# A result buffer of its own for the out product, stored by ACT, in a chunked recurrence with a gated convolution behind it

## The chip, the core and the metric

The kernel runs on one core of a Trainium2 chip. The core has five engines, each with an instruction stream that it works through in order: TensorE (PE, with its weight loads shown apart as PEld), VectorE (DVE), ScalarE (ACT), GpSimd (POOL) and SyncE (SP). Transfers between the chip's memory and the core's, and inside the core's memory, are issued by SP, ACT or POOL and carried by 16 DMA engines. The metric is the device time of one execution in microseconds (us), lower is better.

## The reference, cut to what matters

```python
# B, H, S, D = 4, 8, 768, 40
for t in range(S):
    y[:, :, t] = einsum('bhd,bhde->bhe', r_t, state)
    Sa = einsum('bhde,bhe->bhd', state, a_t)
    state = state * w_t - outer(Sa, b_t) + outer(v_t, k_t)
x = y.transpose(0, 2, 1, 3).reshape(B, S, 320)
gate = sigmoid(causal 5-tap convolution of x along S, per channel)
out = (gate * (x @ w_val)) @ w_out          # (B, S, 320)
```

All data is fp32. A recurrence over 768 steps for 32 heads, and behind it, per time step, a convolution with a sigmoid and two 320 x 320 products.

## The kernel before

**The recurrence** is cut into 24 chunks of 32 steps. A chunk c first has work that needs only its inputs (loads `ew`, scans, the matrices `am`, a triangular solve on DVE for four chunks at a time, lines 427 to 462). Then comes the serial part, chunk after chunk: `u0` on PE (lines 512 to 520) needs the state of the chunk before; ACT copies it into `ub` (523); `ut` and `u` on PE (525 to 533); ACT evacuates them into `vu` and `w` (536, 540); `g` on PE (544); the products `ysa` and `ysb` (553); DVE takes the new state out of them (563) and the results y into the buffer `xe` (577).

**The part behind it** ("the gated part") works on groups of two chunks, 0-1, 2-3, ... to 20-21, and on the single chunks 22 and 23. For group c (named by its first chunk) the steps are: `xd`, twelve transfers inside the core that move y from `xe` into the layout of the products, `xt` (`x_moves`, lines 72 to 80, issued at 705); the convolution `cv` (ACT at 725, DVE at 727) into `ag`; the gate (737 to 742); the product `val` in three parts (PE, lines 90 and 98; DVE at 757 multiplies by the gate); the product `out`, one for each half of the group (108); `os`, ACT's copy of the result out of the accumulator (772); and `store`, the transfer to the output (776). The gated part of a group runs some chunks behind the recurrence, in between its steps.

**Buffers.** `xt` has two halves (`XTW`, lines 287 and 288), used by groups in turn, so the moves of group c write the half that group c - 4 used. The copy `os` of a group writes into that group's own half of `xt`, which its convolution and its product `val` no longer need (line 720, `xo = (XTW, ...)`), and `store` reads it there. `xe` has two halves as well (line 280): before chunk c's y can be written, DVE's copy `new_xe` (572) puts the last four columns of the group before in front, and it has to wait until the moves of group c - 4 have read that half. `td` and `DB` belong to the solve of the first four chunks alone; `DB` lies in the second half of `xt`.

**What sets the order.** Every step is an operation of a `Plan` with an engine, a planned duration, the operations it waits for and a latency. `Plan.order` (lines 166 to 262) places them on the five engines with planned times, and the instructions of each engine are written out in that order. The order is fixed when the kernel is built; on the chip each engine waits at each instruction for the semaphores of its data. So a step that comes late holds everything behind it on its engine. The moves of group c wait in the plan for `("store", pg, 0)` and `("store", pg, 1)` of group pg = c - 4 (line 708). Moves and stores of the groups up to chunk 22 stand on POOL, 560 ns planned for a move, 850 for a store, 2200 for landing; those of chunk 23 partly on SP (line 707). A semaphore that tells that a transfer has landed is one of eight that the transfers of POOL use in turn, and of eight others that those of SP and ACT share in turn; before one is used again the transfer that used it last has to have landed.

```python
xo = (XTW, gi % 2 * 680) if tail < 0 else (fk[tail], 0)
...
op(("os", c, j), "ACT", ac(DM), om, osc)
...
op(("store", c, j), mq[0], mq[2], [("os", c, j)], store, 2200)
```

Of the kernel before, what the change touches and what calls it, by code (L numbers as in the profile page):

```python
# [9 lines left out]
F32 = mybir.dt.float32  # L10
# [6 lines left out]
B, H, S, D = 4, 8, 768, 40  # L17
C = 32
P16 = 16
ER = 104  # L20
DM = 320
# [11 lines left out]
TWO = 1  # L33
# [11 lines left out]
def ac(n):  # L45
    return 154 + 0.833 * n
# [106 lines left out]
class Plan:  # L153
# [6 lines left out]
    def op(self, name, eng, dur, deps, fn, lat=None, give=None):  # L160
        assert name not in self.ops, name
        self.ops[name] = [eng, dur, list(deps), fn, LAT if lat is None else lat]
        if give:
            self.gives[name] = list(give)
# [100 lines left out]
def fast_path(ctx, tc, ins, out, nch, cst, wts, wz, wmx):  # L265


    nc = tc.nc
    V, A, G, T = nc.vector, nc.scalar, nc.gpsimd, nc.tensor
    const = ctx.enter_context(tc.tile_pool(name="const", bufs=1))  # L270
# [3 lines left out]
    ch = ctx.enter_context(tc.tile_pool(name="ch", bufs=2))  # L274
# [12 lines left out]
    XTW = const.tile([128, 2 * 680], F32, name="xt")  # L287
    XT = [XTW[:, i * 680:(i + 1) * 680].rearrange("p (b t) -> p b t", b=10) for i in range(2)]
    DB = XTW[:, 680:1192].rearrange("p (u z s) -> p u z s", z=2, s=C)
    AG = const.tile([128, 2 * 646], F32, name="ag")  # L290
    ind = const.tile([ER, P16, 33], F32, name="ind")
    ern = const.tile([ER, P16, C], F32, name="er")
# [9 lines left out]
    st_ = {}  # L302
    plan = Plan()
    op = plan.op

    sg, groups = [], []
    c = 0
    while c < nch:
        n = min(nch - c, 4)
        sg.append((c, n))  # L310
        c += n
    c = 0
    while c < nch:
        n = 2 if c + 2 < nch else 1
# [8 lines left out]
    def B2(nm, c):  # L323
        return (nm, c, 0), (nm, c, 1)
# [16 lines left out]
    op("bz", "POOL", 1100, [], lambda: G.memset(UB, 0.0))  # L341
    op("nz", "POOL", 3000, [], lambda: [G.memset(x, 0.0) for x in NB + [DB, Q1]])
    op("ez", "SP", 2400, [("load", 6)], lambda: dma(RE.rearrange("p u x -> p (u x)"), ins["re"]), 2500)
# [114 lines left out]
                        in1=maskL.unsqueeze(1).to_broadcast([128, 8, C]), op=ALU.mult)  # L458

    def end2(g):  # L460
        td = st_["td", g] = ch.tile([128, P16, 4, 8], F32, name="td", bufs=1)
        V.transpose(out=td.rearrange("p s c u -> p (s c u)"), in_=st_["x", g][:, 0:P16].rearrange("p s t -> p (s t)"))

    def nblock(c, z):
# [3 lines left out]
    def dblock(c, z):  # L468
        g, c4 = sof[c]
        A.activation(out=DB[:, :, z, 0:P16], in_=st_["td", g][:, :, c4, :].rearrange("p s u -> p u s"), func=AF.Copy, scale=own[:, z:z + 1])  # L470

# [8 lines left out]
    def stage_q2(c, s):  # L480
        for j, i in JI:
            T.matmul(out=s[hr(i), 128 + j * C:160 + j * C], lhsT=DB[hr(i), j].rearrange("p z s -> p (z s)"), rhs=Q1[hr(i), j], start=True, stop=True)

# [98 lines left out]
    for c in range(nch):  # L582
        q = c - NQ
        g, c4 = sof[c]
# [87 lines left out]
    wl = None  # L672
    for i in range(NWT // WB):
# [7 lines left out]
        wl = [("wc", i, 7)]  # L681
# [9 lines left out]
    wl = wl + ["wzc"]  # L691
    prev_gv, prev_out = list(wl), list(wl)
    wv, wo, cw = weights(wts, wz)
    for gi, (c, n) in enumerate(groups):
        L = n * C
        w = B * L
        fk = [KB[(nch + x) % NQ].rearrange("p u d -> p (u d)") for x in range(-NQ, 4 - NQ)]
        tail = gi - len(groups) + 2
        xt = XT[gi % 2] if tail < 0 else fk[tail][:, 0:360].rearrange("p (b t) -> p b t", b=10)
        pg = groups[gi - 2][0] if gi > 1 else -1  # L700
        f = n / 2.0

        def xd(hf, c=c, xt=xt, L=L, last=tail > 0):
            for o, i in x_moves(xt, st_["xe", c], L, hf):
                (nc.sync if last and hf else G).dma_start(out=o, in_=i)  # L705
        last = tail > 0
        mq = ("SP", 860, 650) if last else ("POOL", 560, 850)
        xw = [x for j in range(n) for x in B2("evac_y", c + j)] + wl + [("cv", pg, 4, 0), ("cv", pg, 4, 1), ("cv", pg, 4, 2), ("val", pg, 2), ("store", pg, 0), ("store", pg, 1)]
        if tail >= 0:
            xw = B2("evac_y", c)  # L710
        for hf in range(2):
            op(("xd", c, hf), mq[0] if hf else "POOL", (7 * 560, 4 * mq[1])[hf], xw, lambda hf=hf, xd=xd: xd(hf), 2200)
        xds = [("xd", c, 0), ("xd", c, 1)]
        op(("xd", c), "SP", 1, xds, lambda: None, 2200)
        ag, go = (AG, 640) if tail < 0 else (fk[2 if tail else 3], 320)
        acc, gv = [ag[:, i * go:i * go + 10 * L].rearrange("p (b t) -> p b t", t=L) for i in range(2)]
        gf = ag[:, go:go + 10 * L]
        if tail >= 0:
            prev_gv, prev_out = [], []
        xo = (XTW, gi % 2 * 680) if tail < 0 else (fk[tail], 0)  # L720

        def cv(i, k, xt=xt, L=L, acc=acc):
            q = slice(4 * k, min(4 * k + 4, 10))
            if i == 0:
                A.mul(out=acc[:, q], in_=xt[:, q, 0:L], mul=cw[:, k, 0:1])  # L725
            else:
                V.scalar_tensor_tensor(out=acc[:, q], in0=xt[:, q, i:i + L], scalar=cw[:, k, i:i + 1], in1=acc[:, q],  # L727
                                       op0=ALU.mult, op1=ALU.add)
        for k in range(3):
            for i in range(5):  # L730
                op(("cv", c, i, k), "DVE" if i else "ACT", 70 + (270 if k < 2 else 135) * f + 45, ([("cv", c, i - 1, k)] if i else xds + wl + prev_gv), lambda i=i, k=k, cv=cv: cv(i, k))

        parts = [(0, 4, (0,)), (4, 8, (1,)), (8, 10, (2,))] if c + n == nch else [(0, 10, (0, 1, 2))]
        for i, (q0, q1, ks) in enumerate(parts):
            f_ = f * (q1 - q0) / 10
            a_, g_ = acc[:, q0:q1], gv[:, q0:q1]
            op(("abs", c, i), "ACT", 90 + 535 * f_, [("cv", c, 4, k) for k in ks] + prev_out, lambda a_=a_, g_=g_: A.activation(out=g_, in_=a_, func=AF.Abs))
            op(("gexp", c, i), "ACT", 90 + 535 * f_, [("abs", c, i)], lambda g_=g_: A.activation(out=g_, in_=g_, func=AF.Exp, scale=-1.0))
            op(("gln", c, i), "ACT", 90 + 535 * f_, [("gexp", c, i)], lambda g_=g_: A.activation(out=g_, in_=g_, func=AF.Ln, bias=1.0))
            op(("max", c, i), "DVE", 70 + 670 * f_, [("gln", c, i)],  # L740
               lambda a_=a_, g_=g_: V.scalar_tensor_tensor(out=a_, in0=a_, scalar=0.0, in1=g_, op0=ALU.min, op1=ALU.subtract))
            op(("gate", c, i), "ACT", 90 + 535 * f_, [("max", c, i)], lambda a_=a_: A.activation(out=a_, in_=a_, func=AF.Exp))
        gates = [("gate", c, i) for i in range(len(parts))]
        prev_gv, vm = [], []
        vx = [w, w, w // 2]
        late = c + n == nch

        when = [("u0", c + 3), ("u", c + 3), ("ysb", c + 3, 1), ("u0", c + 4), ("ysb", c + 4, 1)]
        for m in range(3):
            def val(m=m, c=c, xt=xt, L=L, vx=vx):  # L750
                val_mms(nc, slot(("val", c, m))[:, 0:vx[m]], wv, xt, m, L)
            op(("val", c, m), "PE", (1450 if m < 2 else 820) * f, xds + wl + vm + ([] if late else gates + [when[m]]), val, give=[("gv", c, m)])
            vm = [("val", c, m)]
        for m in range(3):
            def gvm(m=m, c=c, L=L, acc=acc, gv=gv, vx=vx):
                q = slice(4 * m, min(4 * m + 4, 10))
                V.tensor_tensor(out=gv[:, q], in0=slot(("val", c, m))[:, 0:vx[m]].rearrange("p (b t) -> p b t", t=L),  # L757
                                in1=acc[:, q], op=ALU.mult)
            op(("gv", c, m), "DVE", dv(256 * f if m < 2 else 128 * f, 1), [("val", c, m)] + gates, gvm)
            prev_gv.append(("gv", c, m))  # L760
        om = []
        prev_out = []
        for j in range(n):
            def outm(j=j, c=c, n=n, gf=gf):
                out_mms(nc, slot(("out", c, j))[:, 0:DM], gf, wo, j, n)
            nm = ("out", c, j)
            op(nm, "PE", 1980, prev_gv + om + ([] if late else [when[3 + j]]), outm, give=[("os", c, j)])
            om = [nm]
            prev_out.append(nm)

            def osc(j=j, c=c, xo=xo):
                A.copy(out=xo[0][:, xo[1] + j * DM:xo[1] + (j + 1) * DM], in_=slot(("out", c, j))[:, 0:DM])  # L772
            op(("os", c, j), "ACT", ac(DM), om, osc)

            def store(j=j, c=c, n=n, L=L, xo=xo, last=last):
                (nc.sync if last else G).dma_start(out=out[j * B // n:(j + 1) * B // n, c * C:c * C + L], in_=xo[0][:, xo[1] + j * DM:xo[1] + (j + 1) * DM])  # L776
            op(("store", c, j), mq[0], mq[2], [("os", c, j)], store, 2200)

    A.preload_act_table_set("natural_log_exp_and_others")
    E_ = mybir.EngineType  # L780
# [168 lines left out]
```

## Time and profile before

| | us |
|---|---|
| time, median of 3 runs (lowest to highest) | 543.69 (542.23 to 549.13) |
| the profiled execution's own time | 543.18 |
| its span in the trace | 541.3 |
| PE busy | 423.7 |
| DVE busy | 378.6 |
| ACT busy | 316.1 |
| POOL busy | 103.4 |

The span is the time from the first instruction of the trace to the last; the rest of the execution's own time lies around it. Busy time counts no waiting and no issuing of loads by SP. The rows below are whole lines of the profile's page and of answers from the trace. In a timeline a row gives the start, the length, the engine, the line, what was done and how often; in brackets stands the idle time of that engine just before, and what ended it. In the chain of work that ended last, read backwards from the end, each piece is what the next one waited for.

### The profile page before, as it was taken

Reading aid. Unit: us, or ns where it says so; the run is one execution under the profiler, and the core shown is the slowest. Engines: PE = TensorE matmul, PEld = TensorE weight load, DVE = VectorE, ACT = ScalarE, POOL = GpSimd, SP = SyncE. Lnnn points to the kernel's source line nnn. Section 1 sums busy time; section 2 is a strip of 40 time slices with the busy share of each in tenths; the row PEclk is TensorE's granted clock in tenths of the full one; section 3 lists DMA queues with packets and bytes.
Section 4 is the critical chain, followed back from the end, with each engine's and each line's share of the span. In section 5 each row is a group of like instructions: output and inputs, shape, how many; then the busy total and the mean of one; then the engine's idle time right before and its main releaser. Section 6 shows DMA issues by size and latency. Waiting matters only on the chain.

```text
span 541.3 us, 22177 instructions
## 1 busy us (share of the span) xinstructions
PE 423.7 (78%) x9769; PEld 364.2 (67%) x9769; DVE 378.6 (70%) x935; ACT 316.1 (58%) x644; POOL 103.4 (19%) x187
## 2 busy tenths in 40 slices
PE   4707669879769979897983996985987988998790
PEld 3707669778759768777872876774876766776660
DVE  4548946887999988796994695994795746443430
ACT  3636455657867769685684485676464527562530
POOL 3000000040310140032031023013014051338410
PEclk8766756888869999897996898997999697999696
DMA  8855733474664646647355526441252352341101
GB/s 179 199 134 135 188 85 90 100 172 111 152 152 99 146 118 136 154 112 164 86 130 133 145 49 154 87 113 29 78 105 60 66 124 59 96 90 35 37 17 38
DMA packets 24262, 58.96 MB, mean 109 GB/s; under 512 B 10953, under 2 KB 15215, under 8 KB 21665
## 3 DMA queue, kind: packets, MB, share of 16 engines
q1 hardware_dynamic: 13169, 49.52, 39.1%
q0 software_dynamic: 10992, 7.97, 6.3%
q8 instruction: 78, 1.28, 1.1%
q14 instruction: 23, 0.19, 0.1%
HBM read 49.25 MB, written 3.93 MB: 98 GB/s over the span
## 4 chain that ended last, share of the span: by engine, by line
PE 42%; DMA 18%; issue 17%; DVE 11%; ACT 6%; POOL 5%; POOLq 0%; ACTq 0%; DVEq 0%
DMA out<-xt 6%; PE pf L90 5%; PE pc L553 4%; PE pf L389 4%; DMA xt<-xe 4%; PE pf L108 4%; DMA ew<-in_ew 4%; PE pf L419 4%; PE pc L532 4%; PE pf L544 4%; POOL xt L705 4%; PE pc L515 3%; PE pc L519 3%; PE pc L528 3%; DMA ag<-in_wts 1%
## 5 line engine op out<-in xcount | busy, mean ns | idle before, releaser
L705 POOL DMA_DIRECT2D xt<-xe x132 | 68.0, 521 | 199.9 <-DVE tm L443 113.7
L727 DVE SCALAR_TENSOR_TENSOR ag<-xt,wts,ag 128x256 f32<-128x256 f32 (+1 forms) x132 | 53.6, 431 | 10.7 <-ACT ag L725 10.6
L776 POOL DMA_DIRECT2D out<-xt x22 | 18.2, 827 | 218.7 <-ACT xt L772 211.6
L389 PE MATMUL pf<-kb,qb 104*64 104x64 f32 x768 | 34.8, 260 | 30.7 <-DVE kb L384 22.8
L389 PEld LDWEIGHTS pf<-kb,qb 104*64 104x64 f32 x768 | 31.9, 172 | 33.0 <-ACT er L356 16.0
L445 DVE TENSOR_TENSOR x<-x,tm 128x58 f32<-128x58 f32 (+9 forms) x164 | 51.4, 314 | 0.6
L443 DVE TENSOR_TENSOR tm<-x 128x58 f32<-128x58 f32 (+9 forms) x164 | 51.3, 313 | 0.6
L108 PE MATMUL pf<-wts,ag 128*128 128x320 f32 x132 | 47.6, 482 | 1.0 <-DVE ag L757 1.0
L544 PE MATMUL pf<-rb,vu 104*64 104x64 f32 x768 | 33.0, 248 | 17.6 <-DVE ak L408 12.3
L544 PEld LDWEIGHTS pf<-rb,vu 104*64 104x64 f32 x768 | 29.2, 159 | 22.2 <-DVE ak L408 12.7
L540 ACT COPY w<-pc 32x640 f32<-32x640 f32 x48 | 32.9, 685 | 17.4 <-PE pc L532 16.9
L351 DVE TENSOR_TENSOR_SCAN lam<-ew,ind 104x528 f32<-104x528 f32 x24 | 30.0, 1248 | 16.8 <-DMA ew<-in_ew 16.7
L532 PE MATMUL pc<-ub,T 64*32 64x80 f32 x768 | 37.4, 254 | 5.3 <-issue 5.3
L553 PE MATMUL pc<-re,s 40*40 40x72 f32 x1472 | 33.1, 231 | 8.3 <-ACT s L422 4.6
L523 ACT ACTIVATE ub<-pc,cst 128x320 f32<-128x320 f32 x48 | 22.7, 522 | 28.0 <-PE pc L519 28.0
L532 PEld LDWEIGHTS pc<-ub,T 64*32 64x32 f32 x768 | 31.9, 121 | 7.8 <-issue 6.5
L380 ACT ACTIVATE qb<-qa,cst 104x512 f32<-104x512 f32 x48 | 32.5, 714 | 7.4 <-DVE qa L377 7.3
L503 ACT ACTIVATE rb<-rv,cst 104x512 f32<-104x512 f32 x48 | 34.5, 719 | 1.9 <-DMA rv<-in_rv 1.6
L553 PEld LDWEIGHTS pc<-re,s 40*40 40x40 f32 x1472 | 27.1, 117 | 12.5 <-ACT s L422 5.0
L553 PE MATMUL pc<-w,kbt 64*40 64x72 f32 x1536 | 33.3, 232 | 1.9 <-DVE w L547 1.1
L419 PE MATMUL pf<-cst,kb 104*128 104x104 f32 x192 | 28.7, 290 | 7.2 <-DVE kb L384 4.3
L528 PE MATMUL pc<-T,ub 64*40 64x32 f32 x1536 | 23.5, 212 | 13.1 <-issue 11.9
(119 smaller groups left out, 952.3 us busy)
## 6 DMA issues: line engine op xcount, KB each, us to landing
ew<-in_ew SPq DMA_DIRECT2D x24, 838.5 KB
rv<-in_rv SPq DMA_DIRECT2D x24, 624.0 KB
w<-in_vw SPq DMA_DIRECT2D x48, 144.0 KB
va<-in_va SPq DMA_DIRECT2D x24, 160.0 KB
out<-xt POOLq DMA_DIRECT2D x22, 160.0 KB, 7.0
xt<-xe POOLq DMA_DIRECT2D x66, 42.5 KB, 5.0
ag<-in_wts SPq DMA_DIRECT2D x5, 323.0 KB
re<-in_re SPq DMA_DIRECT2D x1, 468.0 KB
```

The source lines that it names most:

```text
L108: T.matmul(out=ps, lhsT=gv[r, q * L:q * L + 128], rhs=wo[k][r], start=(k == 0), stop=(k == 2))
L389: T.matmul(out=s[hr(i), j * 64:j * 64 + 64], lhsT=QB[c % NQ][:, pj(j, i)].rearrange("p z t -> p (z t)"), rhs=st_["kb", c][:, pj(j, i)].rea ...
L419: T.transpose(out=s[:, b * 128:b * 128 + ER], in_=src[:, u:u + 2].rearrange("p i f -> p (i f)"), identity=ident[0:ER, 0:ER])
L443: V.tensor_tensor(out=tv, in0=x[:, :, j:j + 1, r].to_broadcast(sh), in1=x[:, :, 0:j, j:j + 1].to_broadcast(sh), op=ALU.mult)
L445: V.tensor_tensor(out=x[:, :, 0:j, r], in0=x[:, :, 0:j, r], in1=tv, op=ALU.subtract)
L503: A.activation(out=st_["rb", c][:, :, z], in_=st_["rv", c][:, 0], func=AF.Copy, scale=ownz[:, z:z + 1])
L528: T.matmul(out=PC[0][hr(z, 40), i, j * C:j * C + C], lhsT=UB[hr(i), j, z], rhs=st_["T", c][hr(i), j], start=True, stop=True)
L532: T.matmul(out=PC[1][i * 64 + 32:i * 64 + 64, j // 4, j % 4 * 80:j % 4 * 80 + 80], lhsT=st_["T", c][hr(i), j], rhs=UB[hr(i), j].rearrange( ...
L544: T.matmul(out=s[hr(i), j * 64:j * 64 + 64], lhsT=st_["vu", c][:, pj(j, i)].rearrange("p x t -> p (x t)"), rhs=st_["rb", c][:, pj(j, i)].r ...
L553: T.matmul(out=PC[g][hr(z, 40), i, j % 4 * 72:j % 4 * 72 + 72], lhsT=l[hr(i, k), j * 2 + z], rhs=rhs[hr(i, k), j * 2 + z], start=start and ...
L705: (nc.sync if last and hf else G).dma_start(out=o, in_=i)
L727: V.scalar_tensor_tensor(out=acc[:, q], in0=xt[:, q, i:i + L], scalar=cw[:, k, i:i + 1], in1=acc[:, q], op0=ALU.mult, op1=ALU.add)
```

## The change

`os` gets a buffer `OS` of its own, with one half for each chunk of a group, used by every group of two chunks; a group's copy waits for the store of the same half of the group before (`po`). All stores are issued by ACT, planned at 400 ns, where they were on POOL (the last one on SP). The moves no longer wait for stores. `td` moves into the first half of `xt`, and so the first group's moves wait for its last readers (`db`), the second group's for the last reader of `DB` (`q2`).

```diff
+    OS = const.tile([128, 2 * DM], F32, name="os")
...
-        td = st_["td", g] = ch.tile([128, P16, 4, 8], F32, name="td", bufs=1)
+        td = st_["td", g] = XTW[:, 0:512].rearrange("p (s c u) -> p s c u", s=P16, c=4)
...
-        xw = [... + wl + [("cv", pg, 4, 0), ("cv", pg, 4, 1), ("cv", pg, 4, 2), ("val", pg, 2), ("store", pg, 0), ("store", pg, 1)]
+        xw = [... + wl + [("cv", pg, 4, 0), ("cv", pg, 4, 1), ("cv", pg, 4, 2), ("val", pg, 2)]
+        if gi == 0:
+            xw += [("db", x, z) for x in range(sg[TWO][0]) for z in range(2)]
+        if gi == 1:
+            xw += [("q2", sg[TWO][0] - 1)]
...
-        xo = (XTW, gi % 2 * 680) if tail < 0 else (fk[tail], 0)
+        xo = (OS, 0) if tail < 0 else (fk[tail], 0)
+        po = groups[gi - 1][0] if gi and tail < 0 else -1
...
-            op(("os", c, j), "ACT", ac(DM), om, osc)
+            op(("os", c, j), "ACT", ac(DM), om + [("store", po, j)], osc)
...
-                (nc.sync if last else G).dma_start(out=out[...], in_=xo[0][...])
-            op(("store", c, j), mq[0], mq[2], [("os", c, j)], store, 2200)
+                A.dma_start(out=out[...], in_=xo[0][...])
+            op(("store", c, j), "ACT", 400, [("os", c, j)], store, 2200)
```

The order of POOL's instructions around one group, before: four moves that end a group's twelve, the two stores (`out<-xt`, line 776) of the group two back, and the first moves of the next group. DMASW0 to DMASW7 are POOL's eight landing semaphores.

```order
L705 DMA xt<-xe 40x272 [waits DMASW3_49]
L776 DMA out<-xt 2x64x320 [waits DMASW4_49,Activation_49]
L776 DMA out<-xt 2x64x320 [waits DMASW5_49,Activation_49]
L705 DMA xt<-xe 40x272 [waits DMASW4_49,DMASW6_49,DVE_49,PE_49]
L705 DMA xt<-xe 40x272 [waits DMASW7_49]
L705 DMA xt<-xe 8x272 [waits DMASW0_49]
L705 DMA xt<-xe 8x272 [waits DMASW5_49,DMASW1_49,PE_49]
```

The same place now:

```order
L706 DMA xt<-xe 40x272 [waits DMASW7_49]
L706 DMA xt<-xe 40x272 [waits DVE_49,DMASW0_49,PE_49,Activation_49]
L706 DMA xt<-xe 40x272 [waits DMASW1_49]
L706 DMA xt<-xe 8x272 [waits DMASW2_49]
L706 DMA xt<-xe 8x272 [waits DMASW3_49,PE_49,Activation_49]
```

The two stores are gone, and with them the waits of the first and of the fourth move for the stores' own landing semaphores (DMASW4 and DMASW5 before). What is left are waits for DVE, PE and ACT, the readers of that half of `xt`, and for moves eight places back.

ACT around the two result copies of one group in the second half of the program, before (lines 772 `os`, 540 and 536 evacuations of the recurrence, 503 and 507 work on loaded `rv`, 523 the copy into `ub`):

```order
L536 COPY vu<-pc_112 104x2x8x32
L772 COPY xt<-pf_116 128x320
L540 COPY w<-pc_113 32x16x40 x2
L503 ACTIVATE rb<-rv,cst 104x16x32
L507 COPY vu<-rv 104x16x32
L503 ACTIVATE rb<-rv,cst 104x16x32
L772 COPY xt<-pf_117 128x320
L510 COPY re<-rv 104x16x32
```

A like place now, with a store (line 782) behind each copy (778; 423 and 511 are lines 422 and 510 of before, 524 is 523):

```order
L778 COPY os<-pf_118 128x320
L782 DMA out<-os 2x64x320
L511 COPY re<-rv 104x16x32
L423 COPY kbt_93<-pf_115 128x320
L778 COPY os<-pf_116 128x320
L423 COPY s_103<-pf_118 128x320
L782 DMA out<-os 2x64x320
L423 COPY s_103<-pf_115 128x320
L524 ACTIVATE ub<-pc_113,cst 128x8x40 x2
```

ACT's stream has 24 stores more; 10 of them have an evacuation or copy of the recurrence (lines 511, 423 for `s`, 524, 537) right behind them. Since the planner places everything anew, the order on PE, DVE and ACT differs too from the second chunk on; each engine's set of instructions is otherwise the same, but for some of PE's filler products (line 795).

## Rows read from the trace of the kernel before

**Rows 1.** The page's first part: busy time, share of the span and number of instructions of each engine.

```profile
PE 423.7 (78%) x9769; PEld 364.2 (67%) x9769; DVE 378.6 (70%) x935; ACT 316.1 (58%) x644; POOL 103.4 (19%) x187
```

**Rows 2.** The chain of work that ended last, summed by line (the page's fourth part).

```profile
DMA out<-xt 6%; PE pf L90 5%; PE pc L553 4%; PE pf L389 4%; DMA xt<-xe 4%; PE pf L108 4%; DMA ew<-in_ew 4%; PE pf L419 4%; PE pc L532 4%; PE pf L544 4%; POOL xt L705 4%; PE pc L515 3%; PE pc L519 3%; PE pc L528 3%; DMA ag<-in_wts 1%
```

**Rows 3.** The same chain in order of time, around 262 and from 272 us on: start, length, what.

```profile
261.78 0.95 PE pf L98 x12
...
272.22 0.43 ACT xt L772
272.66 0.28 issue
272.94 8.29 DMA out<-xt
...
281.84 6.63 DMA xt<-xe
288.47 0.28 issue
288.75 6.62 DMA xt<-xe
...
295.44 0.06 DVE xe L572
```

**Rows 4.** Timeline of POOL, two stretches: moves and stores as issued.

```profile
269.13 0.83 POOL L776 DMA_DIRECT2D out<-xt  x1 [22.35 <-ACT xt L772]
272.94 0.83 POOL L776 DMA_DIRECT2D out<-xt  x1 [2.98 <-ACT xt L772]
276.25 1.58 POOL L705 DMA_DIRECT2D xt<-xe  x3 [2.48 <-DVE x L445]
281.84 4.10 POOL L705 DMA_DIRECT2D xt<-xe  x8 [4.00 <-DMA out<-xt]
288.75 0.51 POOL L705 DMA_DIRECT2D xt<-xe  x1 [2.81 <-DMA xt<-xe]
...
354.86 0.83 POOL L776 DMA_DIRECT2D out<-xt  x1 [4.62 <-ACT xt L772]
356.15 1.58 POOL L705 DMA_DIRECT2D xt<-xe  x3 [0.47 <-PE pc L553]
365.70 4.61 POOL L705 DMA_DIRECT2D xt<-xe  x9 [7.97 <-PE pc L532]
```

**Rows 5.** Who waited for whom: waiting engine and line, releaser, us in total, times, longest.

```profile
DVE xe L572 <- DMA xt<-xe: 19.0, 5, 7.8
ACT ag L725 <- DMA xt<-xe: 6.5, 3, 3.9
```

**Rows 6.** The same view for 255 to 505 us alone.

```profile
ACT kbt L725 <- DMA kbt<-xe: 6.7, 2, 3.5
```

**Rows 7.** Timeline of PE at five places, with PE's idle time before each.

```profile
298.78 1.97 PE L544 MATMUL pf<-rb,vu 104*64 104x64 f32 x32 [6.89 <-DVE ak L408]
...
373.65 1.98 PE L544 MATMUL pf<-rb,vu 104*64 104x64 f32 x32 [5.39 <-DVE ak L408]
...
418.30 1.35 PE L515 MATMUL pc<-va,akb 64*64 64x40 f32 x32 [1.83 <-DVE xe L577]
...
448.85 1.97 PE L544 MATMUL pf<-rb,vu 104*64 104x64 f32 x32 [3.33 <-ACT vu L536]
...
503.12 1.20 PE L553 MATMUL pc<-re,s 40*40 40x72 f32 x32 [4.60 <-ACT s L422]
```

**Rows 8.** Timelines of DVE and ACT just ahead of four of these places.

```profile
371.95 0.19 DVE L572 COPY xe<-xe 104x64 f32<-104x64 f32 x1 [4.82 <-DMA xt<-xe]
...
415.22 0.19 DVE L572 COPY xe<-xe 104x64 f32<-104x64 f32 x1 [3.86 <-DMA xt<-xe]
...
445.77 0.51 ACT L725 ACTIVATE ag<-xt,wts 128x256 f32<-128x256 f32 x1 [3.88 <-DMA xt<-xe]
...
500.81 0.40 ACT L725 ACTIVATE kbt<-kbt,wts 128x128 f32<-128x128 f32 x1 [3.53 <-DMA kbt<-xe]
```

**Rows 9.** Timelines of PE, DVE and POOL: the last part of a product `val` (line 98) at 341 us, the last y of chunk 22 (line 577), and POOL's store and moves around it.

```profile
341.63 0.43 PE L98 MATMUL pf<-xt,wz 64*64 64x128 f32 x4
...
483.61 0.41 DVE L577 TENSOR_TENSOR xe<-pc,lam 104x256 f32<-104x256 f32 x1
...
478.18 0.83 POOL L776 DMA_DIRECT2D out<-xt  x1 [3.95 <-ACT xt L772]
482.53 1.58 POOL L705 DMA_DIRECT2D xt<-xe  x3 [3.52 <-DVE ag L741]
485.42 4.61 POOL L705 DMA_DIRECT2D xt<-xe  x9 [1.30 <-issue]
490.02 7.51 POOL L705 DMA_DIRECT2D kbt<-xe  x12
```

**Rows 10.** Issues by line 776: ns of one, shortest, median and longest, first and last start; POOL's and SP's (SPq); and how long the stores took from issue to landing.

```profile
L776 POOL DMA_DIRECT2D out<-xt x22: 813/827/846, 183.0 to 524.7; - x22
L776 SPq DMA_DIRECT2D out<-kbt x1: 629/629/629, 528.3 to 528.3; - x1
...
DMA to landing us min/median/max: 5.8/6.9/10.3
```

**Rows 11.** SP's issues of loads at line 321, in the same form.

```profile
L321 SPq DMA_DIRECT2D w<-in_vw x48: 310/413/1032, 3.5 to 472.6; - x48
L321 SPq DMA_DIRECT2D ew<-in_ew x24: 307/314/751, 0.8 to 324.7; - x24
```

**Rows 12.** ACT's waits for PE before the copy into `ub`, in the view of waits over the whole span.

```profile
ACT ub L523 <- PE pc L519: 28.0, 18, 4.8
```

**Rows 13.** Timeline: PE's last product from `DB` (line 482), and POOL's first moves; then POOL's stores with the shortest distances, two of each half.

```profile
94.85 0.23 PE L482 MATMUL pf<-ak,xt 64*64 64x32 f32 x2
...
112.40 4.27 POOL L705 DMA_DIRECT2D xt<-xe  x8 [107.63 <-DVE tm L443]
...
497.52 0.82 POOL L776 DMA_DIRECT2D out<-xt  x1
504.54 0.81 POOL L776 DMA_DIRECT2D out<-xt  x1 [6.21 <-ACT xt L772]
...
517.28 0.83 POOL L776 DMA_DIRECT2D out<-xt  x1 [3.45 <-ACT xt L772]
524.73 0.82 POOL L776 DMA_DIRECT2D out<-xt  x1 [6.62 <-ACT xt L772]
```

More of the change, by code (lines that the diff above doesn't have):

```diff
@@ L707, in fast_path @@
         mq = ("SP", 860, 650) if last else ("POOL", 560, 850)
-        xw = [x for j in range(n) for x in B2("evac_y", c + j)] + wl + [("cv", pg, 4, 0), ("cv", pg, 4, 1), ("cv", pg, 4, 2), ("val", pg, 2), ("store", pg, 0), ("store", pg, 1)]
+        xw = [x for j in range(n) for x in B2("evac_y", c + j)] + wl + [("cv", pg, 4, 0), ("cv", pg, 4, 1), ("cv", pg, 4, 2), ("val", pg, 2)]
+        if gi == 0:
+            xw += [("db", x, z) for x in range(sg[TWO][0]) for z in range(2)]
+        if gi == 1:
+            xw += [("q2", sg[TWO][0] - 1)]
         if tail >= 0:
@@ L772, in osc @@
                 A.copy(out=xo[0][:, xo[1] + j * DM:xo[1] + (j + 1) * DM], in_=slot(("out", c, j))[:, 0:DM])
-            op(("os", c, j), "ACT", ac(DM), om, osc)
+            op(("os", c, j), "ACT", ac(DM), om + [("store", po, j)], osc)
             def store(j=j, c=c, n=n, L=L, xo=xo, last=last):
-                (nc.sync if last else G).dma_start(out=out[j * B // n:(j + 1) * B // n, c * C:c * C + L], in_=xo[0][:, xo[1] + j * DM:xo[1] + (j + 1) * DM])
-            op(("store", c, j), mq[0], mq[2], [("os", c, j)], store, 2200)
+                A.dma_start(out=out[j * B // n:(j + 1) * B // n, c * C:c * C + L], in_=xo[0][:, xo[1] + j * DM:xo[1] + (j + 1) * DM])
+            op(("store", c, j), "ACT", 400, [("os", c, j)], store, 2200)
     A.preload_act_table_set("natural_log_exp_and_others")
```

## The prediction

> **What bounds the kernel now.** I read the shares first. PE is busy 78% of the span, DVE 70%, ACT 58%, POOL 19% [rows 1]: no engine is full, and the one that this change unloads is the emptiest. So the question is who waits. The chain of waits, summed by line, holds three entries that are no arithmetic: landing of `out<-xt` 6%, landing of `xt<-xe` 4%, issue of the moves by POOL 4% [rows 2]. That is 14% of 541.3, some 76 us, in which the end of the program hangs on stores and moves. It is no price yet: the chain names one path, and beside it PE has other work to do.
>
> In order of time the chain shows the mechanism once in full [rows 3]. ACT's result copy of group 4 ends at 272.65, POOL issues the store at 272.94, it lands 8.29 us later, then the moves of group 8 go on at 281.84, the last of them is issued at 288.75 and lands 6.62 us later, and at 295.44 DVE can do line 572, the copy at the head of chunk 12's `xe`. POOL's timeline says the same from its side [rows 4]: three moves after the store, then 4.00 us of waiting for the store to land, eight moves, a wait for a move's own semaphore, the last move. At 354.86 it is worse: store, three moves, 7.97 us of nothing, nine moves.
>
> What stands behind late moves shows in the waits: DVE's line 572 waits 19.0 us for moves in 5 waits, ACT's first convolution step (725) 6.5 us in 3 [rows 5], and its copy for the single chunks 6.7 us in 2 [rows 6]. All three are in-order engines on which the recurrence's own steps stand behind the waiting one, so PE feels it.
>
> **The change part by part.**
>
> *Moves no longer wait for stores.* The price is what PE loses, since PE has the most work and its order is fixed. Five idle times of PE have a late move behind them [rows 7], each with the move's wait just ahead of it on DVE or ACT [rows 3, 8]: 6.89 at 298.78 (behind DVE's 295.44), 5.39 at 373.65 (behind 371.95), 1.83 at 418.30 (behind 415.22), 3.33 at 448.85 (behind ACT's 445.77) and 4.60 at 503.12 (behind ACT's 500.81). The sum is 22.0 us. The waits of DVE and ACT themselves, 19.0 + 6.5 + 6.7 = 32.2 [rows 5, 6], are the upper bound: PE may have been slowed at places where it shows no idle time. The lower bound is 0, if moves come as late for another reason; that is a rival below. I take 22.0.
>
> Do the moves come early enough? They now wait for the last readers of that half of `xt`, of which the third part of `val` is the last. For group 4 it ended at 262.73 [rows 3], and the moves that had to follow went on at 281.84: 19 us to gain where 7.84 were lost. For group 8 it ended at 342.06 [rows 9], and the moves that POOL issued from 365.70 on [rows 4] could have gone 23 us earlier where 4.82 were lost. A planner that places `val` some us later than before does not use that up. At 503.12 the late moves are those of chunk 22, which have no store of their own half to wait for; they stand behind group 20's in POOL's queue, issued at 490.02 though chunk 22's y was there at 484.02 [rows 9]. Group 20's moves waited for the store of 478.18, and with them out of the way chunk 22's go 6.0 us earlier; that covers the 4.60.
>
> What is late next: the moves still take 1.58 + 4.10 + 2.81 + 0.51 = 9.0 us from the first issue to the last [rows 4] and 6.62 to land [rows 3], and the convolution then waits for PE and DVE, not for POOL.
>
> *24 stores on ACT.* POOL's 0.83 us an issue [rows 10] goes away from an engine that is 19% busy, worth nothing by itself. No row shows ACT issuing a transfer. The nearest are SP's: 0.63 for the one store on SP [rows 10], 0.31 to 1.03 for loads [rows 11]. I take 0.63, a store of the same size. If all 24 held the path, 24 x 0.63 = 15.1 us; the lower bound is 0, all of them in ACT's own idle time (42% of the span). By the order now, 10 of the 24 have a step of the recurrence right behind them: 10 x 0.63 = 6.3. ACT waits for PE before `ub` 18 times, 28.0 us in all [rows 12], so about half of these issues fall into time in which ACT would have stood still: 3 us. Without that cover it is 6.3. The store also has to wait for the end of ACT's own copy (0.43 us [rows 3]) where it stands right behind it; that is in the rival "slower".
>
> *The copy waits for the store of the group before.* The nearest two stores of the same half are 19.8 us apart (497.52 and 517.28 [rows 13]); the longest landing was 10.3 [rows 10]. Nothing, with 9 us to spare.
>
> *`td` in `xt`, first moves behind `db` and `q2`.* The last product that reads `DB` ran at 95.1, the first move at 112.40, held by DVE [rows 13]. Nothing. The last stores move from POOL and SP to ACT, one behind the other: at most one issue, 0.63, at the end; it is in the 15.1 above.
>
> *The planner's new order.* It moves steps of all engines; what that is worth no row tells. The largest single wait in [rows 7] that an order's choice could make or unmake is 6.89, so I put 0 with 7 us to either side.
>
> **Sum.** 543.18 - 22.0 + 3 = 524.2 against the profiled execution's own time, which lies 0.5 below the median of the three runs; I say **524**.
>
> One rule speaks against all this. The Trainium skill ("DMA: Bandwidth & Descriptors", section "Issuing engines are not separate DMA queues") says that transfers issued by different engines share the same 16 DMA engines, and that issuing from more of them saves just the sequencer's time. By that rule POOL is spared 22 x 0.83 = 18.2 us that nobody waited for, and the kernel stays where it is. The trace agrees that POOL's issuing time is not scarce; but it shows POOL's queue holding moves behind a store's landing, which is not bandwidth.
>
> **Rivals.**
>
> *Only the issuing time is saved (0.09).* The stores and moves are hidden by other work, or the gain is eaten: 543.2 + 3 = 546. For it: POOL's 19% [rows 1]. Against it: PE's idle times sit right behind DVE's and ACT's waits for moves [rows 7, 8].
>
> *The next wait takes half of it (0.15).* The moves come 4 to 9 us earlier but the readers of `xt` or the move's own landing (6.62, twice in a row [rows 3]) hold DVE's line 572 nearly as long. Then perhaps the store's landing alone is saved where PE saw it: half of 22.0, so 543.2 - 11 + 3 = 535. Against it are the 19 and 23 us above.
>
> *ACT becomes the place that holds the recurrence (0.08), slower.* Each store waits for ACT's own copy and is issued in line: 0.43 + 1.03 (the longest issue on SP [rows 11]) = 1.46 us, 24 times, 35.0 us, all on the path: 543.2 - 22.0 + 35.0 = 556. It decides from 24 h - 22.0 = 11 on, that is h = 1.4 us for each store on the path. A store that has to wait for a load of SP with the same landing semaphore would do the same. For it: ACT is at 58% and stands between all PE steps of the recurrence. Against it: ACT's waits before `ub` [rows 12].
>
> **How the numbers follow.** My forecast, moves early and ACT's stores mostly covered, has 0.68. Its own range: all 32.2 with no cost, 511, to 22.0 less 7 for the order and less 6.3 for uncovered issues, 534. A range for 8 in 10 takes in the half-way rival at 535 and stops short of 546: 511 to 541. What is left out is the rule (0.09), the slower case (0.08) and a few hundredths below. Two per cent of 543.7 is 10.9, about what a measurement of this kernel can tell from no change: under 532.8 is faster, over 554.6 slower. The forecast lies under it but for its upper edge: 0.66, and some 0.04 of the half-way case: faster 0.70. Within: the rest of that case, the rule's, the forecast's edge, a little of the last: 0.23. Slower 0.07.
>
> **What the new profile would show.** Right: DVE's line 572 waits no more than 4 us in all for moves; POOL's timeline has twelve moves without a gap of 4 us or more behind three of them; PE's five idle times are gone; the three entries of the chain fall from 14% to below 5%. ACT's stores show some 0.6 us each. Wrong: line 572 still waiting 10 us or more (the half-way rival), or idle times of PE of 2 us and more that end with ACT's `ub`, `vu` or `s` behind a store (the slower one). What would make the number wrong with the mechanism right: PE losing elsewhere what it gains, by an order that puts the gated part's products ahead of the recurrence's, or ACT's issue costing twice what SP's does.

## The result, and the profile after

| | before | after |
|---|---|---|
| median of the comparison (4 runs each) | 546.39 | 526.75 |
| lowest to highest | 542.23 to 549.13 | 520.06 to 535.21 |
| the profiled execution's own time | 543.18 | 520.06 |
| its span | 541.3 | 518.2 |

The ratio of after to before is 0.955, with an interval of 0.941 to 0.970: faster by 3 to 6%. The forecast was 524. Executions that take over 1.5% longer than the fastest of the same kernel are left out of the ratios here and below but not out of the medians, and of the profiles of "buffer alone" and "stores issued by POOL", which come from such executions, only waits and landings are read, not the spans.

The busy times of PE, DVE and ACT, and the sum by line of the chain that ended last:

```profile
PE 423.7 (82%) x9743; PEld 363.7 (70%) x9743; DVE 379.1 (73%) x935; ACT 315.6 (61%) x644; POOL 84.1 (16%) x164
...
PE pc L554 9%; PE pf L90 8%; PE pf L108 7%; PE pf L390 6%; PE pc L533 5%; PE pf L545 5%; PE pf L420 5%; DMA ew<-in_ew 4%; PE pc L516 4%; PE pc L520 4%; PE pc L529 3%; DMA xt<-xe 2%; PE pf L98 2%; POOL xt L706 2%; DMA ag<-in_wts 2%
```

The same work is done in less waiting: PE, DVE and ACT are as busy as before [rows 1], and POOL has lost the stores' issues. In the chain, the groups' stores are gone, and moves hold 2% + 2% where stores and moves together held 14% [rows 2]. (Lines have moved: 572 is now 573, 725 is 731, 705 is 706, 553 is 554, 776 is 782.)

Who waited for transfers, to be held against [rows 5], from the view of waits over the whole span (engine, line, releaser: us in total, times, longest). The first line is of the kernel before, the other two of the changed one:

```profile
ACT kbt L725 <- DMA kbt<-xe: 11.9, 5, 3.5
...
DVE xe L573 <- DMA xt<-xe: 3.0, 2, 1.7
...
ACT kbt L731 <- DMA kbt<-xe: 5.3, 3, 4.2
```

DVE's wait for moves has gone from 19.0 to 3.0, and ACT's wait before the convolution of a group, 6.5 before, has no row any more. ACT's wait for the single chunks is left, 5.3 where it was 11.9; the 6.7 of [rows 6] are the part of it from 255 to 505 us.

POOL's timeline, four of the moves' places, to be held against [rows 4]; in brackets POOL's idle time before and what ended it:

```profile
282.91 5.13 POOL L706 DMA_DIRECT2D xt<-xe  x10 [37.96 <-PE pf L98]
291.95 1.02 POOL L706 DMA_DIRECT2D xt<-xe  x2 [3.90 <-DMA xt<-xe]
325.53 6.21 POOL L706 DMA_DIRECT2D xt<-xe  x12 [32.56 <-DVE ak L409]
356.60 6.21 POOL L706 DMA_DIRECT2D xt<-xe  x12 [24.86 <-ACT vu L537]
```

Twelve moves now go in one row, or with one pause of 3.90 us for the semaphore of an earlier move; nothing waits for a store.

Where the time went is read from the windows, cut at the first product of chunks 1, 12 and 23. Columns: stretch and length; busy time and number of instructions of PE, PE's weight loads, DVE, ACT and POOL; the granted clock of TensorE, DMA share, GB/s. Before:

```profile
97.90:277.60 179.70, 155.15 (x4176) 134.60 (x4171) 157.06 (x399) 128.94 (x262) 31.10 (x57) 0.91 0.56 129
277.60:486.00 208.40, 170.57 (x4196) 143.26 (x4196) 141.80 (x352) 121.76 (x235) 47.79 (x87) 0.89 0.41 96
486.00:541.30 55.30, 36.39 (x505) 27.43 (x505) 17.91 (x60) 16.44 (x41) 20.39 (x33) 0.82 0.14 32
```

After:

```profile
102.20:297.10 194.90, 164.24 (x4180) 142.06 (x4176) 159.32 (x396) 131.17 (x264) 31.07 (x60) 0.83 0.54 129
297.10:472.20 175.10, 160.37 (x4162) 134.13 (x4160) 139.28 (x352) 119.20 (x234) 38.20 (x75) 0.97 0.41 100
472.20:518.20 46.00, 33.04 (x506) 24.46 (x505) 17.70 (x60) 15.99 (x42) 10.77 (x18) 0.89 0.15 36
```

So the 23.1 us between the spans are a sum of opposite signs: the head 102.20 - 97.90 = +4.3, the first eleven chunks +15.2, the next eleven -33.3, the end -9.3. The gain sits from chunk 12 on, where nearly all of the waits for late moves lay (all but 1 us of DVE's 19.0, all of ACT's), and it is 42.6, not 23; a loss ahead of it takes 19.5 back. The experiments had to say whether gain and loss belong to the same cause.

### The profile page after: what moved, and what is told of

Same layout as the page of the kernel before. It is cut to its first block, busy times and chain, and to the rows that moved or that the text cites. A ratio compares the mean times of both kernels' runs of the same rounds, so it can differ in the third digit from the quotient of the medians.

```text
span 518.2 us, 22135 instructions
## 1 busy us (share of the span) xinstructions
PE 423.7 (82%) x9743; PEld 363.7 (70%) x9743; DVE 379.1 (73%) x935; ACT 315.6 (61%) x644; POOL 84.1 (16%) x164
## 3 DMA queue, kind: packets, MB, share of 16 engines
q0 software_dynamic: 4864, 4.12, 3.8%
q10 hardware_dynamic: 3124, 3.93, 2.4%
HBM read 49.25 MB, written 3.93 MB: 103 GB/s over the span
## 4 chain that ended last, share of the span: by engine, by line
PE 60%; DVE 12%; ACT 9%; DMA 9%; issue 7%; POOL 2%; DVEq 0%; POOLq 0%; ACTq 0%
PE pc L554 9%; PE pf L90 8%; PE pf L108 7%; PE pf L390 6%; PE pc L533 5%; PE pf L545 5%; PE pf L420 5%; DMA ew<-in_ew 4%; PE pc L516 4%; PE pc L520 4%; PE pc L529 3%; DMA xt<-xe 2%; PE pf L98 2%; POOL xt L706 2%; DMA ag<-in_wts 2%
## 5 line engine op out<-in xcount | busy, mean ns | idle before, releaser
L390 PE MATMUL pf<-kb,qb 104*64 104x64 f32 x768 | 36.6, 268 | 26.5 <-DVE kb L385 21.8
L390 PEld LDWEIGHTS pf<-kb,qb 104*64 104x64 f32 x768 | 33.2, 179 | 29.7 <-ACT er L357 15.0
L554 PE MATMUL pc<-w,kbt 64*40 64x72 f32 x1536 | 34.7, 238 | 11.5 <-issue 11.5
L554 PEld LDWEIGHTS pc<-w,kbt 64*40 64x40 f32 x1536 | 29.9, 123 | 14.0 <-issue 13.0
L529 PE MATMUL pc<-T,ub 64*40 64x32 f32 x1536 | 23.1, 209 | 15.4 <-issue 10.5
L564 DVE TENSOR_TENSOR st<-pc,lam 104x320 f32<-104x320 f32 x46 | 22.4, 486 | 17.0 <-PE pc L554 12.3
L545 PE MATMUL pf<-rb,vu 104*64 104x64 f32 x768 | 32.2, 246 | 2.2 <-ACT s L423 1.1
L529 PEld LDWEIGHTS pc<-T,ub 64*40 64x40 f32 x1536 | 19.8, 127 | 20.1 <-issue 12.6
L108 PEld LDWEIGHTS pf<-wts,ag 128*128 128x128 f32 x132 | 22.2, 194 | 15.9 <-issue 8.3
## 6 DMA issues: line engine op xcount, KB each, us to landing
xt<-xe POOLq DMA_DIRECT2D x66, 42.5 KB, 3.0
```

Source lines behind the costliest of these rows:

```text
L108: T.matmul(out=ps, lhsT=gv[r, q * L:q * L + 128], rhs=wo[k][r], start=(k == 0), stop=(k == 2))
L390: T.matmul(out=s[hr(i), j * 64:j * 64 + 64], lhsT=QB[c % NQ][:, pj(j, i)].rearrange("p z t -> p (z t)"), rhs=st_["kb", c][:, pj(j, i)].rea ...
L529: T.matmul(out=PC[0][hr(z, 40), i, j * C:j * C + C], lhsT=UB[hr(i), j, z], rhs=st_["T", c][hr(i), j], start=True, stop=True)
L545: T.matmul(out=s[hr(i), j * 64:j * 64 + 64], lhsT=st_["vu", c][:, pj(j, i)].rearrange("p x t -> p (x t)"), rhs=st_["rb", c][:, pj(j, i)].r ...
L554: T.matmul(out=PC[g][hr(z, 40), i, j % 4 * 72:j % 4 * 72 + 72], lhsT=l[hr(i, k), j * 2 + z], rhs=rhs[hr(i, k), j * 2 + z], start=start and ...
```

## The experiments

Twelve runs, on three chips: the first four on one, then four, then four. Each ratio is to the kernel before on the same chip.

**The store's issue alone moves to ACT**, the results stay in `xt`, all in the order of before:

```
-                (nc.sync if last else G).dma_start(out=out[...], in_=...)
+                A.dma_start(out=out[...], in_=...)
```

> The order of before, results still copied into the group's half of xt; only the issue of the stores goes from POOL to ACT. Theory W (moves lose time because they wait for a store's landing in the same half): the moves still wait for that landing, only POOL's queue is free; DVE's line 572 still waits 10 us or more for moves; time 533 to 545. Theory Q (the queue: stores must leave POOL): 520 to 528. Theory O (the planner's new order makes the gain): 543 or a little more.

Ratio 0.976 [0.969, 0.982]. The view of waits of this kernel:

```profile
DVE xe L572 <- DMA xt<-xe: 20.9, 6, 5.8
...
POOL xt L705 <- DMA out<-xt: 31.0, 6, 11.6
```

POOL no longer issues a store, yet its moves still wait 31.0 us for stores to land, because the results lie in their half of `xt`, and DVE waits for moves as long as before in total (20.9 against 19.0). Still it gains 2.4%. At the three places where PE stood behind DVE's wait, the wait is shorter: 4.10, 3.83 and 1.20 us where it was 7.8, 4.82 and 3.86; at two others, in chunk 10 and in the last chunk, it is longer (5.54 and 5.81 where it was 0.96 and 1.53). The waits in total and the median (534.89) are what theory W expects; the gain fits a queue that no longer stands at a store whose result ACT has not finished, and the next run shows that queue by itself.

**The buffer alone**, stores still issued by POOL, order of before (`td` has to go into `xt` to make room, as in the change):

```
+    OS = const.tile([128, 2 * DM], F32, name="os")
...
-        xo = (XTW, gi % 2 * 680) if tail < 0 else (fk[tail], 0)
+        xo = (OS, 0) if tail < 0 else (fk[tail], 0)
```

> The order of before, results in a buffer of their own (td in xt to make room), stores still issued by POOL, so moves stand behind stores in POOL's queue but need not wait for their landing. Theory W: most of the gain, line 572 waits under 6 us, 522 to 532. Theory Q: 538 to 546. Theory O: 543.

Ratio 0.965 [0.956, 0.974]. Waits:

```profile
POOL out L777 <- ACT os L773: 197.9, 13, 36.9
...
POOL xt L706 <- DMA out<-os: 24.5, 6, 6.1
...
DVE xe L573 <- DMA xt<-xe: 10.2, 3, 3.5
```

The moves' data no longer depend on a store, and DVE's wait is halved, not gone. What is left comes through POOL's queue: POOL stands 197.9 us in all at stores whose copy ACT has not done, with moves behind them (how much of this time held a move whose data were there, the view does not tell), and its moves wait 24.5 us more for stores to land. Since the results are elsewhere now, what still ties a move to a store is the landing semaphore, which POOL's transfers use in turn. The median, 532.34, lies at the edge of theory W's range, but the 10.2 us are not under 6 and half of the gain of both parts is missing: the queue counts too.

**Both, in the order of before**: the two edits above together, without the planner's new order.

> The whole change in buffers and queues, but every operation in the order that the planner gave before. Theory W and theory Q: at or below the changed kernel, 512 to 525, since the early part is not reordered. Theory O: 540 to 546.

Ratio 0.929 [0.923, 0.935], span 506.8: 2.6% of the time before better than the changed kernel's 0.955. DVE's line 573 has no wait for moves any more. The windows of this kernel, cut as above:

```profile
97.80:278.60 180.80, 155.40 (x4172) 134.97 (x4168) 157.27 (x399) 128.90 (x262) 30.68 (x60) 0.91 0.56 130
278.60:460.60 182.00, 162.73 (x4195) 137.40 (x4194) 142.08 (x351) 121.19 (x236) 38.02 (x75) 0.96 0.46 109
460.60:506.80 46.20, 33.08 (x506) 24.46 (x505) 17.77 (x60) 16.18 (x42) 10.74 (x18) 0.90 0.13 32
```

The first stretch stays what it was (+1.1 us). The other two shrink by 26.4 and 9.1, together 35.5. PE's idle time in them falls from 37.83 + 18.91 = 56.7 to 19.27 + 13.12 = 32.4, by 24.3. The other 11.2 are PE's busy time, 206.96 before and 195.81 now, with the same products: they run shorter, since the granted clock rises from 0.89 to 0.96 and from 0.82 to 0.90. So the changed kernel's loss in the first eleven chunks does not come with the mechanism; it comes with the new order.

**The changed kernel with its stores issued by POOL** (SP for the last ones, as before), order of after:

> The changed kernel with its order, buffers and no wait for stores, but POOL issues the stores where ACT did. Theory W and theory O: as the changed kernel, 518 to 532, a few us less if ACT's issues had cost something. Theory Q: 538 or more.

Ratio 0.984 [0.978, 0.991], 3% above the changed kernel. In either order, then, it costs 3 to 4% to leave the stores with POOL when the buffer is there (0.965 against 0.929; 0.984 against 0.955). Neither theory's range holds the median, 536.31. And what costs the 3% in the new order is not seen: DVE's line 573 waits 2.6 us for a transfer in this kernel's profile, and POOL's moves wait 4.4 us in all for stores. What is longer is PE's stopping ahead of line 554, which has no releaser (more on such stops at the end); 13.3 us in the changed kernel, and here:

```profile
PE pc L554 <- issue: 24.1, 10, 4.0
```

A rival is left here. POOL's stores differ from ACT's not in their place alone: they are cut into smaller packets. The profile's page for the transfers of POOL before (moves and stores), then for POOL's moves and ACT's stores after (packets, MB, share of the DMA engines' time):

```profile
q0 software_dynamic: 10992, 7.97, 6.3%
...
q0 software_dynamic: 4864, 4.12, 3.8%
...
q10 hardware_dynamic: 3124, 3.93, 2.4%
```

POOL's stores take 10992 - 4864 = 6128 packets, ACT's 3124. No run moves the stores out of POOL's stream and keeps their packets, so what of the 3 to 4% is the queue and what the packets is not separated. For the queue stand, in the old order, the moves' 24.5 us of waits for stores.

**Twice as many issues on ACT**: both parts in the order of before, each store of a two-chunk group issued as two halves, so 22 more issues.

```
+                if n == 2:
+                    for h in range(2):
+                        A.dma_start(out=out[j * 2 + h:j * 2 + h + 1, ...], in_=xo[0][h * 64:h * 64 + 64, ...])
```

> As the run with both parts in the old order (506.67), but each store of a group of two chunks is issued by ACT in two halves: 22 issues of about 0.52 us more, 11.4 us of ACT's time. If ACT's issues lie in its idle time: 506 to 511. If they hold the recurrence, as the term of 3 to 6.3 us for 24 of them says: 509 to 513. If all hold the path: 518.

Ratio 0.939 [0.933, 0.945], span 509.5. It has to be held against the same kernel on other chips, which gave 0.929 on one and 0.943 on another (below): 22 issues cost 1.0% or nothing. The upper value is 5.4 us, 0.25 us an issue, though an issue takes ACT 0.52 in the changed kernel and 0.60 for a half here. The rows, the changed kernel's first (ns of one issue, shortest, median and longest; first and last start):

```profile
L782 ACTq DMA_DIRECT2D out<-os x22: 521/522/1153, 197.9 to 501.6; - x22
...
L779 ACTq DMA_DIRECT2D out<-os x44: 473/596/1373, 182.6 to 495.3; - x44
```

**Another order with the old waits, another with the new.** The plan's duration for a store is changed from 850 to 900 in the kernel with both parts and the old waits, and from 400 to 520 in the changed kernel; each shifts the planner's choices, nothing else.

```
-        mq = ("SP", 860, 650) if last else ("POOL", 560, 850)
+        mq = ("SP", 860, 650) if last else ("POOL", 560, 900)
...
-            op(("store", c, j), "ACT", 400, [("os", c, j)], store, 2200)
+            op(("store", c, j), "ACT", 520, [("os", c, j)], store, 2200)
```

> Buffers and queues as in the run with both parts in the old order; the planner still believes that moves wait for stores on POOL, but a planned store lasts 900 ns in place of 850, which gives an order of which 81% of PE's rows stand as before. Theory N (any new order from this planner costs some us by chance): 512 to 530. Theory S (the planner's order is worse because it no longer sees the waits): 503 to 511.

> The changed kernel with a planned store of 520 ns on ACT in place of 400, the length that the trace shows; of PE's rows 78% stand as in the changed kernel. Theory N: anything from 505 to 530. Theory S: 518 to 532, as the changed kernel.

Ratios 0.956 [0.948, 0.964] with the old waits and 0.949 [0.942, 0.955] with the new. A planned number that changes by 50 ns, with the waits as they were, gives an order that is 1.8% slower than the kernel with doubled issues on the same chip (0.939), and the intervals do not meet. So a new order can cost without the new waits in the plan. That the new waits cost nothing does not follow: with them, too, every order that was tried is a new one.

**More filler products.** The kernel puts products without use between others on PE; a constant of the planner sets how many. From 67 of them to 143, in the changed kernel, to see whether the lower clock of its first half is the cause of the loss:

```
-RHO, CAP, DUM = 0.37, 700, 250
+RHO, CAP, DUM = 0.6, 700, 250
```

> The changed kernel in its own order, with 143 filler products on PE in place of 67. Theory C (what the new order costs is the clock, granted 1.2 GHz from 150 to 177 and 208 to 228 us since PE has too little planned work there): 508 to 518, and these stretches at full clock. If the clock falls for waits that no plan sees: 522 to 532, the stretches as they were.

Ratio 0.972 [0.962, 0.982]: not faster than the changed kernel's 0.955. The first stretch, cut at about the same places:

```profile
97.00:297.00 200.00, 165.72 (x4335) 144.66 (x4332) 159.11 (x391) 130.85 (x265) 30.57 (x60) 0.87 0.53 125
```

The clock did rise there, from 0.83 to 0.87, and to 0.72 and 0.74 in the two stretches that theory C names (150 to 177, 208 to 228), which stand at 0.50 in the changed kernel's profile. The time did not fall: with the added products PE is busy 165.7 us there against 164.2, and idle 34.3 against 30.7. But these two stretches do not hold their clock from one execution to the next: a second profile of the changed kernel (below) has 0.71 and 0.76 in them without an added product, and its first eleven chunks take as long as in the first. So the run says that filler products brought no gain; it does not settle theory C.

**The old order and the changed kernel once more, on one chip, with two variants.** The third lets SP issue the stores of the old-order kernel (`nc.sync.dma_start`); the fourth plans the changed kernel with latencies nearer to what the traces show: 6600 ns for moves to land, 520 and 7000 for a store and its landing.

```
-            op(("xd", c, hf), ..., xw, lambda hf=hf, xd=xd: xd(hf), 2200)
+            op(("xd", c, hf), ..., xw, lambda hf=hf, xd=xd: xd(hf), 6600)
...
-            op(("store", c, j), "ACT", 400, [("os", c, j)], store, 2200)
+            op(("store", c, j), "ACT", 520, [("os", c, j)], store, 7000)
```

> The same kernel as both parts in the old order, beside the changed kernel on one chip: 503 to 511; if its lead over the changed kernel was a matter of chips, within 1% of it.

> The changed kernel once more, beside the old order on one chip: 520 to 530, 2.5 to 4% longer than the old order.

> Both parts in the old order, but SP issues the stores, at the places where ACT did. If ACT's issues cost what the doubled ones did (0.2 us each, some 5 us in all), 500 to 504, as far as SP's loads, which now stand behind stores that wait for ACT's copies, do not come late; if they do, 510 or more with waits for loads on DVE and ACT.

> The changed kernel, planned with latencies of the kind that the trace shows: 6600 ns for a move's landing in place of 2200, 7000 for a store's, 520 for its issue. Theory N (a new order costs or gains by chance): 505 to 530. If wrong latencies were what made the new order bad: at or below 507.

| on this chip | median | ratio |
|---|---|---|
| old order, ACT's stores | 511.04 | 0.943 [0.934, 0.952] |
| changed kernel | 524.23 | 0.954 [0.943, 0.966] |
| old order, SP's stores | 509.39 | 0.934 [0.921, 0.946] |
| changed kernel, other latencies | 514.34 | 0.950 [0.938, 0.961] |

The changed kernel comes out as it did the first time (0.954, 0.955). The old order is ahead again, by 1.1%, but here the intervals overlap, so on one chip the lead is not shown. What is the same each time is where the two differ. The windows, cut as above: old order, then changed kernel.

```profile
98.40:278.20 179.80, 156.33 (x4170) 135.81 (x4168) 156.98 (x399) 128.82 (x262) 30.69 (x60) 0.90 0.56 131
278.20:463.80 185.60, 166.37 (x4195) 140.86 (x4194) 142.09 (x352) 121.30 (x236) 38.02 (x75) 0.94 0.45 106
...
97.30:293.00 195.70, 166.73 (x4182) 145.18 (x4178) 158.41 (x391) 131.71 (x264) 30.56 (x59) 0.83 0.54 129
293.00:462.20 169.20, 159.50 (x4161) 133.85 (x4160) 140.52 (x358) 119.33 (x233) 38.68 (x76) 0.97 0.44 107
```

In both profiles of each kernel the new order takes 14 to 16 us more for the first eleven chunks (194.9 and 195.7 against 180.8 and 179.8), and gives part of it back in the next eleven (175.1 and 169.2 against 182.0 and 185.6). In this pair it gives all of it back: the spans are 508.4 for the changed kernel and 509.9 for the old order.

Whether ACT or SP issues the stores can't be told apart (the intervals overlap); either way they are no longer POOL's. The longer planned latencies bring no order that beats the old one.

## Why the prediction was right, step by step

The time came out 0.5% from the forecast, and the mechanism is the one that it named. Two of its terms were mis-sized in opposite directions and nearly cancel; that the total is so close is luck.

- **Which wait bounds.** Right, and both parts of it are shown. Buffer and queue were named together as what makes moves late; apart they are worth 3.5% and 2.4%, together 7.1% on the same chip and 5.7% on another. Neither does it alone: with the issue alone the data still wait, with the buffer alone the queue does. What of the queue's part belongs to POOL's smaller packets stays open.
- **22.0 us from five idle times of PE.** As a count of idle time it was close: 24.3 less idle from chunk 12 on in the old order, 21.7 of it in the five chunks in which the five places lie. As the gain it was too small: the same products take 11.2 us less, because the granted clock falls behind such idle times, as the trace of before shows (below). The term leaves out that the time around a removed wait becomes cheaper too. The bound of 32.2 was passed as well (35.5, after what ACT's issues cost), but it was also read too small: its 6.7 for the single chunks end at 505 us, and over the whole span that wait is 11.9, which makes the bound 37.4. One of the five places was not won: with both parts in the old order chunk 12 still takes 29.3 us, 30.8 before, since PE there stops elsewhere (3.49 us ahead of line 554 at 300.26); the others give more than their idle time.
- **3 us for ACT's 24 issues.** The size of one was 0.52, predicted 0.63. Doubling them costs between nothing and 0.25 us an issue; if a first issue costs what a second does, 24 cost between nothing and 6 us. The term of 3 is not contradicted, nor the bound of 6.3; nothing nearer is shown.
- **0 ± 7 for the new order.** This was set too favourably. The old order with the same mechanism stands at 0.929 and 0.943 (0.934 with SP's stores), the changed one at 0.955 and 0.954: the order takes 2.6% or 1.1%, 14 or 6 us of 546, the second within the spread. It is the sum of a loss and a gain. The loss is in the first eleven chunks, 194.9 against 180.8 us, 8.8 of it in PE's busy time at a clock of 0.83 against 0.91, 5.3 in idle time; it stands in both profiles of each kernel, and so it is shown to come from the order; from which of its places is not. The gain is from chunk 12 on, 175.1 against 182.0, most of it in chunk 12, which takes 15.0 us in place of 29.3. Of three other orders that the planner made, two (0.956 and 0.949) are behind the old one with its doubled issues on their chip (0.939), the second narrowly; the third (0.950) is not clear of the old one's 0.943, and it has no such loss (180.2 us for the first eleven chunks).
- **`td`, `db` and `q2`, the copy that waits for a store, the end.** No wait of these shows in the profile after; costed at nothing, they cost nothing that shows.

The rivals. *Only the issuing time is saved* (546) fell: moving the issue alone gave 2.4%, where the rule that was weighed ("DMA: Bandwidth & Descriptors" in the Trainium skill, section "Issuing engines are not separate DMA queues") leaves only the sequencer's time, which nobody waited for. The runs do not contradict it on bandwidth; what that section does not speak of is a queue that is worked off in order, where a transfer whose data are late holds those behind it. *The next wait takes half* (535) fell: DVE's 573 waits 3.0 us, not 10. *ACT becomes the place* (556) fell: it needed 1.4 us a store on the path, and some 0.25 at most was found.

Of the signs that were named, all came: line 573 under 4 us, no gap of 4 us behind a store in POOL's row, PE's five idle times gone, 4% in the chain, half a microsecond an issue.

The best versions of those tried have both parts in the old order: 0.929 and 0.943 of before, and 0.934 with SP's stores, against 0.955 and 0.954.

## What to carry to other kernels

Look at what stands behind a transfer in its engine's queue, and not only at whether that engine is busy: POOL was 19% busy, and taking the stores from it gave 2.4% by itself and 3 to 4% with the buffer. Break both ties, the data and the queue; with one left, half of the gain or more was missing (2.4 and 3.5 of 7.1%). When a change also lets a planner make a new order, run the change in the old order too, or a gain of 6 to 7% is taken for one of 4.5%.

## What the runs showed of the hardware

The granted clock fell in or right behind long idle times of PE. The kernel before, windows ahead of and behind the idle times that end at 373.65, 418.30, 448.85 and 503.12:

```profile
366.00:371.00 5.00, 1.79 (x64) 1.56 (x64) 0.69 (x1) 4.83 (x9) 4.29 (x9) 1.00 0.19 52
373.00:382.00 9.00, 8.35 (x154) 7.69 (x156) 6.15 (x13) 4.13 (x8) 0.00 (x0) 0.53 0.27 73
414.00:418.00 4.00, 1.51 (x5) 0.48 (x3) 2.75 (x9) 2.35 (x5) 0.70 (x1) 1.00 0.20 31
419.00:429.00 10.00, 10.00 (x148) 7.41 (x146) 7.76 (x23) 3.97 (x7) 0.00 (x0) 0.50 0.48 101
441.00:445.00 4.00, 2.63 (x99) 1.93 (x98) 0.00 (x0) 0.43 (x1) 3.61 (x8) 1.00 0.45 123
446.00:453.00 7.00, 4.15 (x39) 3.59 (x40) 5.13 (x15) 5.22 (x11) 0.41 (x1) 0.52 0.14 31
497.00:501.00 4.00, 1.51 (x62) 1.28 (x58) 0.35 (x1) 0.47 (x2) 1.34 (x2) 0.99 0.18 26
501.00:511.00 10.00, 6.74 (x112) 6.30 (x113) 5.89 (x17) 7.04 (x14) 2.87 (x5) 0.50 0.17 42
```

The granted clock is the third number from the end of a row: 0.99 to 1.00 (2.4 GHz) ahead, 0.50 to 0.53 (1.2 GHz) behind. In the stretch where these idle times are gone the changed kernel keeps the full clock for 122 us:

```profile
386.00:508.00 122.00, 118.03 (x2740) 95.61 (x2735) 82.69 (x232) 71.87 (x148) 36.76 (x68) 1.00 0.35 83
```

And its own loss in the first eleven chunks shows the same thing the other way: at 148.91 PE had stood for 3.93 us, and the clock is at its lower level behind it, for work that takes longer by that.

```profile
144.03 0.95 PE L554 MATMUL pc<-w,kbt 64*40 64x72 f32 x47
148.91 0.50 PE L554 MATMUL pc<-w,kbt 64*40 64x72 f32 x17 [3.93 <-issue]
...
150.00:175.00 25.00, 18.66 (x311) 16.38 (x311) 21.52 (x60) 14.40 (x28) 6.09 (x12) 0.50 0.36 88
```

What PE waited for there the profile does not name: "issue" means that it shows no releaser. The stop stands inside a run of 64 equal products, after 47 of them, where no new operand begins. The trace holds transfers of kind "instruction", 16 KB each, on a queue of their own; one of them ran from 146.0 to 147.3 us, and PE went on 1.6 us after its end. The page's line for them (number, MB, share):

```profile
q8 instruction: 78, 1.28, 1.1%
```

From chunk 1 on the changed kernel has 13 stops of over 0.3 us without a releaser inside a run of equal products, and each ends 1.2 to 1.8 us after such a transfer has ended. So PE seems to stand there for its next instructions; that is read from the times, and no run tests it, nor why those transfers come late. At line 554 such stops take 13.3 us in the changed kernel's trace, 7.6 in the old-order kernel's with both parts, 2.8 in that of before, but over all lines PE's waits without a releaser are about the same: 27.3, 28.1 and 28.1. They change places with the order; in the first eleven chunks they take 18.8 us in the changed kernel and 15.9 in the old order, which is 2.9 of the 5.3 us of idle time lost there.

How long moves (those of 42.5 KB) take to land differs between kernels without one cause that the runs name: in the median 5.0 us before, 5.9 with the buffer alone, 4.6 with both parts in the old order, 3.0 in the changed kernel. That the stores left the queue is not it, since the changed kernel with POOL's stores has 3.0 too; nor is it the order alone, since the old order with doubled issues has 3.3. It was not followed further.
